# Sums of v on VectorE instead of GpSimd, with a new plan and a new order of the first batch's transposes

## Chip, core and metric

The kernel runs on one core of one Trainium2 chip. The metric is the device time in microseconds of one execution; the figure for a kernel is the median of its runs. A core has five engines that work side by side, each with its own instruction queue that it works off in order: PE (TensorE, matmuls), DVE (VectorE, elementwise work), ACT (ScalarE, activations and copies), POOL (GpSimd) and SP (SyncE, here used to issue DMAs). They wait for one another by semaphores. SBUF is the working memory, PSUM the memory into which PE accumulates.

## What is computed

Two stages follow each other, and only the result of the second leaves the chip. Attention over 8 batches of 3008 tokens, width 256, with 64 columns for the scores:

```python
scores = scale * np.matmul(z, z.transpose(0, 2, 1))   # scale = 1 / S, S = 3008
attn = np.maximum(scores, 0.0) ** 2
x = u * np.matmul(attn, v)                            # [8, 3008, 256]
```

and a feed-forward layer on the 24064 tokens, with an inner width of 2048:

```python
h = x @ w_in
g = h * np.cos(h)
out = g @ w_out
```

The scores of a batch are symmetric, since z meets itself.

## The kernel before, in words

**Tiling.** Tokens are cut into blocks of 128; 24 blocks make a batch (the last has 64 tokens), and 4 blocks make a column of 512 tokens, six columns a batch. `c` is the column whose output is being made, `R` the group of four key blocks that is summed over, `k` a block in a group. A score tile of column c and group R holds 4 x 128 keys by 512 tokens in 16 bits.

**Scores.** `s_visit` makes score tiles in visits of up to three pairs of blocks: `s_matmuls` (line 263) writes two PSUM banks for each pair, ACT takes the positive part (line 299, on diagonal tiles line 280), DVE squares it (line 301, diagonal line 285). As the scores are symmetric, only tiles with R >= c are computed, and the others are turned copies: after the second pair of a tile, `s_squares` issues a DMA transpose on SP's queue (line 308) into a tile "t" of its own. In the first batch, columns 0, 1 and 2 ("direct") are computed whole, without turned copies. `NSLOT` = 18 buffers hold all these tiles; `use` records from when to when each is needed, and `place` assigns the buffers.

**Attention times v.** For the groups in `WSET[c]` (groups 0 to 2, for the last two columns 0 to 3) the product of scores and v goes by a scheme of seven products in place of eight, on halves: `product(b, c, n)` (line 465) uses sums and differences of score quarters, made by DVE in place (`a_sums1`, lines 422 and 424; `a_sums2`, line 434), and sums of v quarters, which lie in `vsum[R]`, four parts for each group (part 0 is read by product 5, part 1 by 6, part 2 by 7, part 3 by 4). `keep` (lines 479 to 490) moves and adds the partial results. The other groups go as plain matmuls, `av_bank` (line 351), and `av_half` adds the last half block (line 328). `finish` multiplies the result by u turned (`turn_u`, line 179, another DMA transpose on SP) and gives x (line 380).

**Sums of v.** `v_sums(b, R)` makes `vsum[R]` once for each batch and group R = 0 to 3 by four GpSimd operations of 256 elements each (lines 391 to 395): part 0 = V12 − V11, part 2 = V22 − V12, part 1 = V22 − part 0, part 3 = V21 − part 1.

**Feed-forward.** `h_quantum` makes 128 rows of h (two matmuls, line 499), the cosine by ACT (line 503), and the product on DVE (line 506). `y_quantum` multiplies by w_out (line 516), ACT copies the result out (line 523) and issues the store. Score visits, h and y share the six PSUM banks of `ps_w`; the two others are the accumulators of the attention.

**Loads.** GpSimd issues all loads of u, v, z and the weights (line 119), each held behind the matmul that stands before it in the plan (`hold`). v comes in three blocks of eight key blocks each, planned 12, 3.2 and 0.8 units before the batch begins.

**The order.** All of it is written out as a list of events `(time, rank, ...)` in a planner's unit; a column takes U = 8 units, a batch 48, and batch b begins at 48 b. Sorting the list gives the order in which the instructions are traced; PE's order is fixed by it (`chain`). The tables at the head say when what is due in a column, in units from its start: `PLAN` (products "P1" to "P7", plain blocks "A" for the first and "B" for the second accumulator), `SUM1` and `SUM2` (first time and step of the score sums), `WADD` and `RADD` (additions of `keep`), `HALF` (from when `av_half` may go), `TSUM` (when the v sums of groups 0 to 3 are due, from the start of the batch). In the first batch the v sums stand at 16 to 19 units. `after(ins, other, NOSYNC)` tells the compiler to put an instruction behind another without a wait.

Of the kernel before, what the change touches and what calls it, by code (L numbers as in the profile page):

```python
# [14 lines left out]
def kernel(  # L15
# [9 lines left out]
    nc = tc.nc  # L25
# [43 lines left out]
    }  # L69
    SUM1, SUM2, WADD, RADD = {0: (-3.9, 0.65), 1: (-3.8, 0.35), 2: (-2.4, 0.3), 3: (-2.9, 0.7), 4: (-3.65, 0.55), 5: (-3.0, 0.75)}, {0: (1.95, 0.02), 1: (1.85, 0.02), 2: (1.95, 0.02), 3: (1.6, 0.02), 4: (2.0, 0.02), 5: (1.85, 0.02)}, {0: 5.26, 1: 4.96, 2: 4.26, 3: 4.36, 4: 4.26, 5: 4.46}, {0: 4.45, 1: 5.75, 2: 4.15, 3: 4.05, 4: 3.55, 5: 4.65}  # L70
    TSUM = [-2.0, -1.9, -0.8, 2.0, 2.5]
    XEND = 4.0
    WSET = {0: [0, 1, 2], 1: [0, 1, 2], 2: [0, 1, 2], 3: [0, 1, 2], 4: [0, 1, 2, 3], 5: [0, 1, 2, 3]}
    HALF = {0: 5.2, 1: 3.9, 2: 3.7, 3: 4.1, 4: 4.2, 5: 4.7}
# [168 lines left out]

    def slot(*key):
        return slots[slot_of[key]].rearrange("p (s k w) -> p s k w", s=K, w=P)
# [24 lines left out]
    def s_squares(b, c, R, p, banks):  # L270
# [30 lines left out]
        nc.vector.tensor_tensor(  # L301
            t.rearrange("p s k w -> p k s w")[:, 2 * p:2 * p + 2], rv, rv, ALU.mult)
        if p == 1:
            fresh[(b, c, R)] = [t[:, :, k, :] for k in range(K)]
            if R > c and not direct(b, R, c):
                tt = slot("t", b, c, R)
                turned[(b, c, R)] = tt
                nc.sync.dma_start_transpose(
                    tt.rearrange("p s k w -> p (s k) w"),
                    t.rearrange("p s k w -> p (s k w)"))  # L310
# [54 lines left out]
    def finish(b, c):  # L365
# [12 lines left out]
        for nh in range(NDH):  # L378
            for x, o, n in parts:
                nc.vector.tensor_tensor(  # L380
                    x[:, nh, :], acc[nh][:, o:o + n], ut[:, nh, o:o + n], ALU.mult)


    def v_sums(b, R):

        j = R * K
        t = vs(b, j // G)
# [350 lines left out]
```

## Time and profile before

| what | before |
|---|---|
| median of 11 runs | 1267.58 us (1264.02 to 1270.7) |
| profiled execution | 1264.8 us, of which the span from first to last instruction is 1263.0 us |
| busy PE / DVE / ACT / POOL | 97% / 84% / 66% / 19% of the span |
| mean granted TensorE clock | 0.982 |
| chain that ended last | PE 91%, DVE 7%, ACT 1%, issue 1% |

A line of the profile names a group of instructions by line, engine, operation and what it writes and reads; "x151 | 95.9, 640 | 2.0" means 151 instructions, 95.9 us busy, 640 ns mean, and 2.0 us that the engine stood idle just before them, with what ended that idle time behind an arrow. Weight loads (PEld) run beside the matmuls. The granted clock is the share of its full clock that PE is allowed at the time.

### The profile page before, as it was taken

The page shows a single profiled execution, that of the slowest core. Times are in us where ns is not written, and L with a number is a line of the kernel's source. Part 1 is how long each engine was busy: PE and PEld are TensorE (multiplying, and loading weights), DVE is VectorE, ACT ScalarE, POOL GpSimd, SP SyncE. Part 2 cuts the span into 40 slices and gives each one's busy share as a digit, 9 for nine tenths or more (in the row PEclk, how much of TensorE's full clock was granted, in tenths as well). Part 3 has the DMA queues.
Part 4 walks back from the last instruction along what each step waited for, and adds up shares of the span by engine and source line. Part 5 has one row for each costly group of instructions (what it writes and reads, how often), then busy time and mean ns, then how long its engine had stood idle before and what let it go on. Part 6 is the DMA issues. An engine that isn't in the chain of part 4 may idle for free.

```text
span 1263.0 us, 23106 instructions
## 1 busy us (share of the span) xinstructions
PE 1227.0 (97%) x8439; PEld 774.1 (61%) x8439; DVE 1056.0 (84%) x1977; ACT 836.1 (66%) x1744; POOL 236.8 (19%) x329
## 2 busy tenths in 40 slices
PE   8999899998999989999999999999999999999999
PEld 3366566664666646666566665666656666566666
DVE  8988878888788887888878888788887888878875
ACT  6767667675666767667667676676766767567655
POOL 4601401014010140101401014010140101400000
PEclk9999899998999989999999998999989999899999
DMA  9997868678687695868867668786696857956401
GB/s 163 180 150 115 127 99 128 109 115 118 103 117 126 115 112 108 124 119 118 127 101 126 108 116 134 100 128 106 111 140 91 136 105 107 140 106 105 81 26 51
DMA packets 484226, 145.02 MB, mean 115 GB/s; under 512 B 432400, under 2 KB 484112, under 8 KB 484112
## 3 DMA queue, kind: packets, MB, share of 16 engines
q1 hardware_dynamic: 356448, 88.73, 43.3%
q0 software_dynamic: 100400, 29.77, 23.7%
q10 hardware_dynamic: 27264, 25.06, 6.1%
q8 instruction: 66, 1.08, 0.4%
q14 instruction: 48, 0.39, 0.1%
HBM read 60.29 MB, written 24.64 MB: 67 GB/s over the span
## 4 chain that ended last, share of the span: by engine, by line
PE 91%; DVE 7%; ACT 1%; issue 1%
PE w L516 25%; PE w L499 25%; PE acc L465 18%; PE acc L351 16%; PE w L263 6%; DVE s L424 3%; DVE g L506 1%; DVE s L301 1%; ACT rt L299 1%; PE acc L328 1%; DVE s L422 0%; PE w L695 0%; ACT zT L224 0%; DVE x L380 0%; DVE s L434 0%
## 5 line engine op out<-in xcount | busy, mean ns | idle before, releaser
L503 ACT ACTIVATE c<-w 128x512 f16<-128x512 f32 x752 | 440.0, 617 | 286.8 <-PE w L499 192.7
L506 DVE TENSOR_TENSOR g<-w,c 128x512 f16<-128x512 f32 x752 | 490.3, 682 | 55.1 <-ACT c L503 53.1
L516 PE MATMUL w<-w_out,g 128*128 128x256 f16 x3008 | 454.5, 275 | 0.0
L499 PE MATMUL w<-x,w_in 128*128 128x512 f16 x1504 | 454.0, 385 | 0.0
L516 PEld LDWEIGHTS <-g 128*128 128x128 f16 x3008 | 297.4, 99 | 197.8 <-issue 9.6
L299 ACT ACTIVATE rt<-w 128x512 f16<-128x512 f32 x489 | 253.2, 615 | 54.4 <-PE w L263 54.4
L351 PE MATMUL acc<-s,v 128*128 128x512 f16 (+1 forms) x1000 | 283.8, 379 | 0.8 <-DVE x L380 0.8
L301 DVE TENSOR_TENSOR s<-rt 128x1024 f16<-128x1024 f16 x254 | 179.1, 711 | 102.3 <-ACT rt L299 101.1
L499 PEld LDWEIGHTS <-w_in 128*128 128x128 f16 x1504 | 148.7, 99 | 69.2 <-issue 3.2
L119 POOL DMA_DIRECT2D ust<-in_u_dram x112 | 81.6, 736 | 566.3 <-PE acc L351 543.2
L465 PE MATMUL acc<-s,vsum 128*128 128x256 f16 (+1 forms) x1208 | 157.9, 270 | 0.9 <-DVE q L481 0.7
L351 PEld LDWEIGHTS <-v 128*128 128x128 f16 x1000 | 93.0, 98 | 84.1 <-issue 34.1
L263 PE MATMUL w<-zT 64*128 64x512 f16 (+3 forms) x684 | 100.4, 365 | 30.0 <-DVE g L506 27.3
L465 PEld LDWEIGHTS <-vsum 128*128 128x128 f16 x1208 | 117.2, 98 | 17.8 <-issue 4.4
L465 PE MATMUL acc<-s,v 128*128 128x256 f16 (+1 forms) x906 | 117.6, 270 | 0.0
L434 DVE TENSOR_TENSOR s<-s,s 128x1024 f16<-128x1024 f16 (+1 forms) x151 | 94.9, 670 | 9.3 <-PE acc L465 8.9
L465 PEld LDWEIGHTS <-v 128*128 128x128 f16 x906 | 85.4, 98 | 20.4 <-issue 12.4
L424 DVE TENSOR_TENSOR s<-s 128x512 f16<-128x512 f16 (+1 forms) x151 | 95.9, 640 | 2.0
L263 PEld LDWEIGHTS <-zT 64*128 64x128 f16 x684 | 26.4, 94 | 86.8 <-issue 73.2
L523 ACT ACTIVATE ob<-w 128x256 f32<-128x256 f32 x188 | 71.2, 378 | 8.0 <-PE w L516 8.0
L380 DVE TENSOR_TENSOR x<-acc,ut 128x64 f16<-128x64 f32 (+7 forms) x178 | 68.8, 428 | 2.4 <-PE acc L351 1.7
L280 ACT ACTIVATE rt<-w 128x512 f16<-128x512 f32 (+3 forms) x176 | 62.8, 451 | 11.5 <-PE w L263 8.3
(38 smaller groups left out, 442.0 us busy)
## 6 DMA issues: line engine op xcount, KB each, us to landing
out_dram<-ob ACTq DMA_DIRECT2D x92, 256.0 KB, 2.2
ust<-in_u_dram POOLq DMA_DIRECT2D x80, 128.0 KB, 4.6
v<-in_v_dram POOLq DMA_DIRECT2D x16, 512.0 KB, 6.5
s<-s SPq DMA_TRANSPOSE x249, 4.4
v<-in_v_dram POOLq DMA_DIRECT2D x8, 448.0 KB, 8.0
zst<-in_z_dram POOLq DMA_DIRECT2D x14, 128.0 KB, 4.9
ust<-in_u_dram POOLq DMA_DIRECT2D x16, 96.0 KB, 4.3
w_in<-in_moe_w_in_dram POOLq DMA_DIRECT2D x4, 256.0 KB, 8.9
```

The costliest lines, as they stand in the source:

```text
L119: hold(nc.gpsimd.dma_start(dst, src))
L263: chain(nc.tensor.matmul(sp[:, s0 * P:], zt[h, R * K + k + 1 - lo, :], zt[h, j0 + s0:j0 + K, :].rearrange("p j w -> p (j w)"), start=True, ...
L299: nc.scalar.activation(rt[:, i, :], banks[k], AF.Relu)
L301: nc.vector.tensor_tensor(t.rearrange("p s k w -> p k s w")[:, 2 * p:2 * p + 2], rv, rv, ALU.mult)
L351: chain(nc.tensor.matmul(acc[:, 0:wn], vs(b, j // G)[:, j % G, nh * P:(nh + 1) * P], a, start=(start and n == 0), stop=(last and n == len( ...
L424: nc.vector.tensor_tensor(second(b, c, R), s1, quarters(b, c, R, (0, 0)), ALU.subtract)
L434: after(nc.vector.tensor_tensor(dst, src, sub, ALU.subtract).ins, before[-1], NOSYNC)
L465: chain(nc.tensor.matmul(acc[bank][:, cols], lhs[:, k, :], rhs[:, k, :] if old else rhs[:, :, k * P:(k + 1) * P], start=(n in (1, 5) and i ...
L499: chain(nc.tensor.matmul(hp, w_in16[:, k, ft * P:(ft + 1) * P], x[:, k, :], start=(k == 0), stop=(k == NDH - 1)))
L503: nc.scalar.activation(c16, hp, AF.Sin, bias=math.pi / 2.0, scale=inv_s2)
L506: nc.vector.tensor_tensor(gs[(m, ft // FG)][:, ft % FG, :], hp, c16, ALU.mult)
L516: chain(nc.tensor.matmul(ys[m][:, 0:D], gs[(m, f4)][:, ft % FG, ts * P:(ts + 1) * P], w_out16[:, ft, :], start=(ft == 0), stop=(ft == NFT ...
```

## The change

Four things are done together.

1. `v_sums` goes to VectorE, in three operations: parts 0 and 2 come from one operation of 512 elements, parts 1 and 3 from one of 256 each. They stand at new planned points: `TSUM` goes from −2.0, −1.9, −0.8, 2.0 to −2.9, −0.9, −0.8, 3.5 units for the groups 0 to 3.
2. The first batch's score transposes are no longer issued when a tile is done, but as events of their own at times given by `TURNS`, in the order in which later columns read the turned tiles. The lives of the buffers follow.
3. The u transposes of the first three columns of the first batch move to 0.7, 0.8 and 3.0 units (from 1, 5 and 10). In those direct columns, squares and positive parts on VectorE are put behind the last product of the preceding `finish` (`behind`).
4. The tables `PLAN`, `SUM1`, `SUM2`, `WADD`, `RADD` and `HALF` have new values: the same products, blocks and sums at other times.

```diff
...
-    TSUM = [-2.0, -1.9, -0.8, 2.0, 2.5]
+    TSUM = [-2.9, -0.9, -0.8, 3.5, 3.5]
...
-    HALF = {0: 5.2, 1: 3.9, 2: 3.7, 3: 4.1, 4: 4.2, 5: 4.7}
+    HALF = {0: 3.6, 1: 3.2, 2: 3.2, 3: 3.4, 4: 4.5, 5: 4.2}
...
+    TURNS = {(0, 0, 1): None, (0, 0, 2): None, (0, 1, 2): None,
+             (0, 0, 3): 1.0, (0, 0, 4): 2.4, (0, 1, 3): 7.8, (0, 0, 5): 8.0,
+             (0, 2, 3): 14.4, (0, 1, 4): 14.6, (0, 2, 4): 15.8, (0, 1, 5): 20.0,
+             (0, 2, 5): 22.0}
...
-                nc.vector.tensor_scalar_max(rt[:, i, :], banks[k], 0.0)
+                behind(nc.vector.tensor_scalar_max(rt[:, i, :], banks[k], 0.0).ins)
...
+        if direct(b, c, R):
+            behind(ins)
         if p == 1:
             fresh[(b, c, R)] = [t[:, :, k, :] for k in range(K)]
-            if R > c and not direct(b, R, c):
...
+            if R > c and (b, c, R) not in TURNS:
+                turn_s(b, c, R)
+
+    def turn_s(b, c, R):
+        tt = slot("t", b, c, R)
+        turned[(b, c, R)] = tt
+        nc.sync.dma_start_transpose(
+            tt.rearrange("p s k w -> p (s k) w"),
+            halves[(b, c, R)].rearrange("p s k w -> p (s k w)"))
...
+        if direct(b, c, c):
+            ended[:] = [ins]
+
+    ended = []
+
+    def behind(ins):
+
+        if ended:
+            after(ins, ended[0], NOSYNC)
...
     def v_sums(b, R):
 
         j = R * K
-        t = vs(b, j // G)
-        k1, k2 = (slice(j % G + 2 * i, j % G + 2 * i + 2) for i in range(2))
-        d1, d2 = slice(0, P), slice(P, 2 * P)
+        t = vs(b, j // G)[:, j % G:j % G + K, :].rearrange("p (h k) d -> p h k d", h=2)
         o = vsum[R]
-        after(nc.gpsimd.tensor_tensor(o[:, 0], t[:, k1, d2], t[:, k1, d1],
-                                      ALU.subtract).ins, before[-1], NOSYNC)
-        nc.gpsimd.tensor_tensor(o[:, 2], t[:, k2, d2], t[:, k1, d2], ALU.subtract)
-        nc.gpsimd.tensor_tensor(o[:, 1], t[:, k2, d2], o[:, 0], ALU.subtract)
-        nc.gpsimd.tensor_tensor(o[:, 3], t[:, k2, d1], o[:, 1], ALU.subtract)
+        b12, b22 = t[:, :, :, P:2 * P], t[:, 1, :, P:2 * P]
+        left = t[:, 0, :, :].rearrange("p k (d w) -> p d k w", w=P)
+        after(nc.vector.tensor_tensor(o[:, 0:3:2], b12, left, ALU.subtract).ins,
+              before[-1], NOSYNC)
+        nc.vector.tensor_tensor(o[:, 1], b22, o[:, 0], ALU.subtract)
+        nc.vector.tensor_tensor(o[:, 3], t[:, 1, :, 0:P], o[:, 1], ALU.subtract)
...
-            if p == 1 and R > c and not direct(b, R, c):
+            if p == 1 and R > c and TURNS.get((b, c, R), t) is not None:
+                t = TURNS.get((b, c, R), t)
                 use(("t", b, c, R), t + 0.8, t + 2.5)
                 use(("a", b, c, R), t, t + 3)
...
+    for key, t in TURNS.items():
+        if t is not None:
+            at(t, 3.5, lambda key=key: turn_s(*key))
...
-            at(t + c * U + (1 if b or c not in (1, 2) else -3 * c), 0, lambda b=b, c=c: turn_u(b, c))
+            at(t + c * U + (1 if b or c > 2 else (0.7, -7.2, -13.0)[c]), 0, lambda b=b, c=c: turn_u(b, c))
```

The new tables, in part (columns 0 and 5 of `PLAN`, and the times of the sums):

```diff
-        0: [(1.0, 'P1 P5 P2'), (2.35, 'B1'), (2.55, 'P6 B1'), (3.0, 'P7 B1'),
-            (3.4, 'P3'), (4.55, 'A1'), (5.0, 'P4 A1'), (5.4, 'B1'), (6.15, 'B3'),
-            (6.35, 'B2'), (6.55, 'A2'), (7.0, 'A2 B2'), (7.4, 'A5')],
+        0: [(1.0, 'P1 P2'), (1.4, 'P5'), (2.35, 'P6 B1'), (2.55, 'B1'), (3.0, 'P7 B1'),
+            (3.4, 'P3'), (4.55, 'A1'), (4.75, 'A1'), (5.4, 'P4 B2'), (6.15, 'A1 B2'),
+            (6.35, 'A1 B1'), (6.55, 'A2'), (6.75, 'A1'), (7.0, 'A1 B2'), (7.4, 'A3 B1')],
...
-            (3.4, 'P7'), (4.35, 'B1'), (4.75, 'P4 A1'), (5.4, 'A1 B2'), (6.15, 'A2'),
-            (6.35, 'A1'), (7.0, 'A2 B1'), (7.4, 'B1')],
+            (3.4, 'P7 B2'), (4.75, 'A1'), (5.0, 'P4'), (5.4, 'A1 B1'), (6.15, 'A1 B1'),
+            (6.35, 'A2'), (6.75, 'A1'), (7.0, 'B2'), (7.4, 'A1')],
...
-    SUM1: {0: (-3.9, 0.65), 1: (-3.8, 0.35), 2: (-2.4, 0.3), 3: (-2.9, 0.7), 4: (-3.65, 0.55), 5: (-3.0, 0.75)}
+    SUM1: {0: (-3.9, 0.5), 1: (-1.8, 0.4), 2: (-1.9, 0.15), 3: (-2.9, 0.65), 4: (-4.65, 0.65), 5: (-3.0, 0.7)}
-    SUM2: {0: (1.95, 0.02), 1: (1.85, 0.02), 2: (1.95, 0.02), 3: (1.6, 0.02), 4: (2.0, 0.02), 5: (1.85, 0.02)}
+    SUM2: {0: (1.85, 0.02), 1: (1.75, 0.37), 2: (1.85, 0.02), 3: (1.5, 0.02), 4: (1.9, 0.02), 5: (1.75, 0.07)}
```

More of the change, by code (lines that the diff above doesn't have):

```diff
@@ L379, in finish @@
             for x, o, n in parts:
-                nc.vector.tensor_tensor(
-                    x[:, nh, :], acc[nh][:, o:o + n], ut[:, nh, o:o + n], ALU.mult)
+                ins = nc.vector.tensor_tensor(
+                    x[:, nh, :], acc[nh][:, o:o + n], ut[:, nh, o:o + n], ALU.mult).ins
+        if direct(b, c, c):
[4 more added lines that the diff above has]
+            after(ins, ended[0], NOSYNC)
     def v_sums(b, R):
         j = R * K
-        t = vs(b, j // G)
-        k1, k2 = (slice(j % G + 2 * i, j % G + 2 * i + 2) for i in range(2))
-        d1, d2 = slice(0, P), slice(P, 2 * P)
+        t = vs(b, j // G)[:, j % G:j % G + K, :].rearrange("p (h k) d -> p h k d", h=2)
         o = vsum[R]
-        after(nc.gpsimd.tensor_tensor(o[:, 0], t[:, k1, d2], t[:, k1, d1],
-                                      ALU.subtract).ins, before[-1], NOSYNC)
-        nc.gpsimd.tensor_tensor(o[:, 2], t[:, k2, d2], t[:, k1, d2], ALU.subtract)
-        nc.gpsimd.tensor_tensor(o[:, 1], t[:, k2, d2], o[:, 0], ALU.subtract)
-        nc.gpsimd.tensor_tensor(o[:, 3], t[:, k2, d1], o[:, 1], ALU.subtract)
+        b12, b22 = t[:, :, :, P:2 * P], t[:, 1, :, P:2 * P]
[4 more added lines that the diff above has]
+        nc.vector.tensor_tensor(o[:, 3], t[:, 1, :, 0:P], o[:, 1], ALU.subtract)
     def by_key(b, c, R):
```

11 lines of the change are left out of this document (3 added, 8 removed), and 26 rows, old and new, of the table PLAN.

## The prediction

> **What bounds the kernel now.** I read the page first, then the busy time by stretches of the span, then the timeline of a stretch that stood out. The profiled execution took 1264.8 us, its span is 1263.0 us.
>
> ```profile
> span 1263.0 us, 23106 instructions
> ...
> PE 1227.0 (97%) x8439; PEld 774.1 (61%) x8439; DVE 1056.0 (84%) x1977; ACT 836.1 (66%) x1744; POOL 236.8 (19%) x329
> PEclk9999899998999989999999998999989999899999
> ...
> L506 DVE TENSOR_TENSOR g<-w,c 128x512 f16<-128x512 f32 x752 | 490.3, 682 | 55.1 <-ACT c L503 53.1
> ...
> L424 DVE TENSOR_TENSOR s<-s 128x512 f16<-128x512 f16 (+1 forms) x151 | 95.9, 640 | 2.0
> ```
>
> PE is the bound, but two things in these lines are not those of a full PE: its granted clock dips six times, five slices apart, with the dip between the third and the fourth left out, and a VectorE operation of line 424 on 512 16-bit elements takes 640 ns on average, hardly less than line 506 with a 32-bit operand from PSUM. The stretches, cut at the dips and at the place of the missing one, show where PE loses its time (columns: length, busy time of PE, PEld, DVE, ACT and POOL with instruction counts, granted clock, DMA share, GB/s):
>
> ```profile
> 0.00:15.00 15.00, 11.73 (x66) 4.57 (x67) 10.08 (x22) 9.21 (x16) 9.78 (x18) 1.00 1.15 160
> 50.00:70.00 20.00, 17.53 (x96) 8.20 (x95) 19.94 (x37) 14.96 (x31) 10.46 (x14) 1.00 1.47 179
> 128.00:143.00 15.00, 10.10 (x50) 4.79 (x48) 14.24 (x16) 7.02 (x16) 12.06 (x18) 0.77 1.14 143
> 143.00:286.00 143.00, 143.00 (x1022) 93.20 (x1020) 118.92 (x235) 98.30 (x208) 16.14 (x22) 1.00 0.67 112
> 286.00:301.00 15.00, 9.94 (x46) 4.71 (x44) 14.49 (x19) 7.03 (x15) 12.45 (x19) 0.81 1.15 146
> 445.00:460.00 15.00, 10.10 (x50) 4.84 (x48) 14.69 (x19) 7.37 (x16) 12.85 (x19) 0.77 1.30 142
> 604.00:617.00 13.00, 10.02 (x51) 5.08 (x49) 13.00 (x19) 7.06 (x16) 12.51 (x18) 0.87 1.28 184
> 760.00:774.00 14.00, 11.28 (x52) 5.38 (x51) 13.67 (x19) 7.22 (x16) 12.63 (x18) 0.76 1.29 184
> 917.00:931.00 14.00, 11.27 (x51) 5.39 (x50) 13.66 (x19) 7.12 (x15) 12.46 (x18) 0.76 1.30 186
> 1074.00:1088.00 14.00, 10.95 (x49) 5.21 (x48) 13.39 (x18) 7.08 (x15) 12.56 (x18) 0.76 1.22 170
> 1212.00:1263.00 51.00, 47.84 (x360) 34.58 (x357) 30.55 (x48) 27.49 (x55) 0.00 (x0) 1.00 0.14 42
> ```
>
> Inside a batch PE is busy 143.00 of 143.00 us at full clock: nothing is to be won there. The loss sits in the seven stretches where one batch follows another, and there GpSimd is busy 12 to 13 us. The timeline of the first and of the fourth says why:
>
> ```profile
> 128.34 6.36 DVE L424 TENSOR_TENSOR s<-s 128x512 f16<-128x512 f16 x1
> 128.75 1.31 POOL L391 TENSOR_TENSOR vsum<-v 128x256 f16<-128x256 f16 x2
> 131.60 0.39 PE L263 MATMUL w<-zT 64*128 64x512 f16 x1
> 134.49 0.73 POOL L394 TENSOR_TENSOR vsum<-v,vsum 128x256 f16<-128x256 f16 x1
> 134.62 1.15 DVE L301 TENSOR_TENSOR s<-rt 128x1024 f16<-128x1024 f16 x1
> 135.69 2.47 DVE L506 TENSOR_TENSOR g<-w,c 128x512 f16<-128x512 f32 x4
> 136.43 0.86 PE L263 MATMUL w<-zT 64*128 64x384 f16 x2 [4.44 <-DVE g L506]
> ...
> 602.11 0.92 POOL L119 DMA_DIRECT2D v<-in_v_dram  x1 [4.80 <-PE w L263]
> 604.18 4.50 DVE L424 TENSOR_TENSOR s<-s 128x512 f16<-128x512 f16 x1
> 607.11 1.28 POOL L395 TENSOR_TENSOR vsum<-v,vsum 128x256 f16<-128x256 f16 x2
> 607.44 0.39 PE L263 MATMUL w<-zT 64*128 64x512 f16 x1
> 608.64 1.79 POOL L393 TENSOR_TENSOR vsum<-v 128x256 f16<-128x256 f16 x2 [0.25 <-DMA v<-in_v_dram]
> 609.94 0.32 PE L263 MATMUL w<-zT 64*128 64x384 f16 x1 [2.11 <-DVE g L506]
> ```
>
> ```profile
> L424 DVE TENSOR_TENSOR s<-s x151: 377/414/6361, 53.1 to 1209.7; 128x512 f16<-128x512 f16 x119, 128x448 f16<-128x448 f16 x32
> ```
>
> The last row gives shortest, median and longest duration: an operation of 0.41 us lasts 6.36 us while GpSimd works off its sums one after another. In the fourth stretch it ends at 608.68, inside the 0.25 us (608.39 to 608.64) in which GpSimd had no sum because it waited for v. So VectorE gets its operands only when GpSimd pauses. The products of line 506 wait behind it, the score matmuls of line 263 wait for the PSUM buffers that these free, and after the wait the clock is halved (0.76 over 14 us).
>
> On VectorE's waiting, the Trainium skill (SBUF — State Buffer, Who interferes with whom) says that the pair of ports shared by GpSimd and VectorE is an exclusive lock, that an operation with two SBUF inputs needs it, and that the first to start has it for one whole instruction. The trace agrees on the blocking, not on its length: by the page VectorE would wait for one sum at most.
>
> **The change part by part.**
>
> *Sums leave GpSimd.* What goes is the whole chain above. Idle PE in the seven stretches, length less PE busy: 4.90 + 5.06 + 4.90 + 2.98 + 2.72 + 2.73 + 3.05 = 26.3 us. Clock not granted, length times (1 − clock): 3.45 + 2.85 + 3.45 + 1.69 + 3 × 3.36 = 21.5 us. Together 47.9 us. A second count: the seven hold 349 matmuls, which at the 1022 in 143 us of a steady stretch need 48.8 us of their 100, so 51.2 us are lost. The two differ by the mix of matmul sizes; I take 48.
>
> The Trainium skill (TensorE: Matmul & The Clock Gate, What's actually happening) puts the halving behind an idle window of about 3.4 us. Here a wait of 2.11 us was enough, so I count all seven; by the page only the first three would pay, and the two sums would be 26.3 + 9.8 = 36 us.
>
> *Sums come to VectorE.* A group costs one operation of 512 elements and two of 256. The first is bounded by line 424's 0.41 us; the nearest rows for 256 elements are these:
>
> ```profile
> L285 DVE TENSOR_TENSOR s<-rt 128x256 f16<-128x256 f16 x44 | 15.6, 355 | 0.0
> L481 DVE TENSOR_TENSOR q<-acc,p 128x256 f32<-128x256 f32 x37 | 15.3, 413 | 0.0
> ...
> L394 POOL TENSOR_TENSOR vsum<-v,vsum 128x256 f16<-128x256 f16 x32 | 23.5, 744 | 1.4
> ```
>
> L285 (0.36, some of them slowed by GpSimd) is the nearest form; I take 0.30. A group is 0.41 + 2 × 0.30 = 1.0 us against 4 × 0.74 = 3.0 us on GpSimd, and 32 groups are 32 us; if the rows of 128 elements, which no VectorE operation of before reads, make them as slow as operations with 32-bit operands, 0.68 (line 506) + 2 × 0.41 (line 481) = 1.5 us, 48 us in all. VectorE sheds 95.9 − 151 × 0.414 = 33 us of blocking at line 424 alone, so its total stays near 1056 us, under 90% of a shorter span: no bound on average.
>
> Locally it may be one. Of the 14.24 us that VectorE is busy in 128:143, 5.94 are blocking; 8.3 us of work stand against 15 − 8.35 = 6.65 us of PE at full speed. Two groups land at −0.9 and −0.8 units in that place (a unit is a planner's step, 3.3 us: 1263 over 8 × 48), one at −2.9 and one at 3.5. That is a deficit of 8.3 + 2.0 − 6.65 = 3.65 us, if PE could not run ahead at all: 25.6 us over seven. Against it: PE loses nothing in a stretch where VectorE has no idle time either.
>
> ```profile
> 750.00:758.00 8.00, 8.00 (x65) 5.63 (x63) 7.96 (x16) 4.35 (x9) 1.30 (x2) 1.00 0.35 82
> ```
>
> ```profile
> v<-in_v_dram POOLq DMA_DIRECT2D x16, 512.0 KB, 6.5
> ```
>
> ```profile
> 125.58 0.92 POOL L119 DMA_DIRECT2D v<-in_v_dram  x1 [4.12 <-PE acc L351]
> ```
>
> Then a new wait: group R = 2 reads v's second block, issued at 125.58 and landed 6.5 us later, 132.1. PE reached the score visit of −0.8 at 131.60, so VectorE can stand there about 0.5 us (1.1 in the fourth: 602.11 + 6.5 against 607.44), with the next score squares and the products of line 506 queued behind it and PE's six PSUM buffers behind those. I charge both together 0.7 us of PE at each crossing, 5 us, between 0 and 25.6 + slow clock; I stay near the lower end because of the 7.96 row. The group at −2.9 overwrites what product 4 of the last column reads at −3.0: eight matmuls, under 1 us on VectorE, covered as in 750:758.
>
> *GpSimd's queue.* Without sums it issues v's third block on time instead of after 134.49; its readers come over 3 units later. Zero.
>
> *First batch.* Its score transposes and u transposes change places in SP's queue, and VectorE takes the finishing products of a column before the squares.
>
> ```profile
> 39.90 1.46 PE L351 MATMUL acc<-s,v 128*128 128x512 f16 x6 [0.78 <-DVE x L380]
> 40.28 31.07 SPq L308 DMA_TRANSPOSE s<-s  x7
> ...
> 67.72 0.81 PE L465 MATMUL acc<-s,vsum 128*128 128x256 f16 x6 [0.66 <-DVE q L481]
> ```
>
> SP is backed up for 31 us, yet nothing on PE waits for a transpose; what waits is 0.78 us for a finishing product, and 2.5 us in 50:70, where VectorE is busy 19.94 of 20. Four groups of sums (4 us) enter between 40 and 55 us, where GpSimd's stood, and the doubling of line 301 by GpSimd (1.15 for 0.69, as in the row at 134.62) leaves. The held-back transposes, three for column 3 from 14.4 to 15.8 units at 4.4 us each, have 5 units (16 us) before their first reader. I take 0; the ends are −3.3 (both waits gone) and +4 (sums on the path).
>
> *The new order of products, A/V pieces and score sums.* The same matmuls in other places. In-batch waits are nil now, so this can only lose: the longest wait of a product is the 0.66 us at 67.72, and at each of the 45 planned columns (48 less the first three) that would be 30 us. The 143.00 of 143.00 shows how rare such waits are with the present plan; zero, with the 30 us kept for the second rival.
>
> *Sum.* 1264.8 − 48 + 5 = 1222 us for an execution like the profiled one. That one lies 2.8 us under the median of 1267.58, so the median of the changed kernel is 1222 to 1225; I put 1223.
>
> **The rivals.**
>
> *A rest of the stall stays.* VectorE's deficit, its wait for v, or product waits by the new order leave 1.5 to 3 us idle at each crossing. As 2.11 us was enough to lose the clock once, 3.4 us come on top at some: 7 × 1.5 = 10 to 7 × (3 + 2) = 35 us back on 1264.8 − 48 + 2.8 = 1220: 1230 to 1255. For it the 8.3 against 6.65; against it the 7.96 row.
>
> *The sums are not what holds VectorE*, as the order of starts suggests: line 424 began at 128.34, before the first sum at 128.75. Then one sum of 0.7 us per crossing is saved, 5 us, VectorE gains 32 us of work in its idle time, and the time is 1260 to 1267: no change. Against it: the end inside GpSimd's pause at 608.68. The page on the shared ports, taken by its letter, stands with this rival.
>
> *Slower: VectorE waits in order for v's second block.* Price: 7 × (W + 3.4). It equals the 48 us won at W = 3.5 us, so v would have to land 10 us after its issue, or VectorE reach the group 3 us sooner than PE's place for it. At W = 5 the time is 1220 + 59 = 1279. The 6.5 us median speaks against it.
>
> **How the numbers follow.** My forecast 0.75 (1212 to 1231), the rest of the stall 0.18 (1230 to 1255), sums innocent 0.03, slower 0.04. The low end of the range is 1264.8 − 51.2 − 3.3 = 1210; the high end, 1245, takes in two thirds of the second case. About 0.2% is what a measurement can tell here (2.5 us): faster 0.93, same 0.03, slower 0.04.
>
> **What would show it.** Line 424 with no duration above 0.8 us; GpSimd with DMA issues alone; granted clock 1.00 at all crossings; a PE near 98 to 99% of the span. Wrong if a crossing still shows a score matmul that waits over 1.5 us for line 506, if VectorE's first sum of group 2 waits for the DMA of v for over 2 us, or if products wait for VectorE inside batches.

## The result and the profile after

| | before | after |
|---|---|---|
| median | 1267.32 us (1263.02 to 1271.95, 47 runs) | 1226.66 us (1220.01 to 1231.54, 12 runs) |
| ratio after to before | | 0.9681, 95% interval 0.9666 to 0.9696 |
| profiled execution, its granted clock | 1264.8 us, 0.982 | 1221.55 us, 0.997 |

The forecast was 1223 us in a range of 1210 to 1245. The runs of the changed kernel fall into two groups, six at 1220.0 to 1224.7 us with a granted clock of 0.996 to 0.999 and six at 1228.6 to 1231.5 us with 0.993 or 0.994, and the profiled execution is one of the shorter six.

From the page of the changed kernel, the same lines as before. Line numbers have shifted: the score sums of line 424 are now line 444, those of 422 line 442, the products of 506 line 526, the score matmuls of 263 line 270, the squares of 301 line 308, the score transposes of 308 line 320, the u transposes of 179 line 181.

```profile
span 1219.5 us, 23076 instructions
...
PE 1208.8 (99%) x8439; PEld 769.6 (63%) x8439; DVE 1028.1 (84%) x2073; ACT 833.7 (68%) x1744; POOL 145.8 (12%) x201
...
PEclk9989999999999999999999999999999999999999
```

The dips of the granted clock are gone but the one in the third slice, which is the first batch, and PE is 99% busy. The same matmuls take 18.2 us less of busy time (1227.0 to 1208.8), since none of them runs at half clock at a batch's end. The stretches that stood out, cut in the same way (length, busy PE, PEld, DVE, ACT, POOL, granted clock, DMA share, GB/s):

```profile
50.00:70.00 20.00, 15.68 (x70) 6.86 (x69) 14.65 (x28) 12.06 (x24) 4.41 (x7) 0.83 1.35 195
...
128.00:143.00 15.00, 15.00 (x108) 9.46 (x107) 14.59 (x35) 11.92 (x26) 4.46 (x6) 1.00 1.02 136
...
286.00:301.00 15.00, 15.00 (x110) 9.74 (x109) 13.47 (x32) 10.73 (x25) 2.10 (x3) 1.00 1.28 190
```

The first crossing from batch to batch holds 108 matmuls where it held 50, with no idle time and no clock withheld; the other six crossings of this trace, too, have PE busy throughout and a clock of 1.00. The stretch of the first batch, 50:70, went the other way: 70 matmuls where there were 96, and a clock of 0.83 where it was 1.00. The durations of single lines (count, shortest/median/longest in ns):

```profile
L412 DVE TENSOR_TENSOR vsum<-v x32: 412/416/419, 42.1 to 1054.7; 128x512 f16<-128x512 f16 x32
...
L414 DVE TENSOR_TENSOR vsum<-v,vsum x32: 277/281/285, 42.8 to 1056.8; 128x256 f16<-128x256 f16 x32
...
L444 DVE TENSOR_TENSOR s<-s x151: 375/414/427, 53.8 to 1166.2; 128x512 f16<-128x512 f16 x119, 128x448 f16<-128x448 f16 x32
```

A group of sums costs VectorE 0.42 + 2 × 0.28 = 0.98 us (line 415 has the same median as line 414), and line 444, whose longest was 6361 ns, has none above 427.

### The profile page after: what moved, and what is told of

Read it like the earlier page. It is cut to its first block, busy times and chain, and to the rows that moved or that the text cites. A ratio compares the mean times of both kernels' runs of the same rounds, so it can differ in the third digit from the quotient of the medians.

```text
span 1219.5 us, 23076 instructions
## 1 busy us (share of the span) xinstructions
PE 1208.8 (99%) x8439; PEld 769.6 (63%) x8439; DVE 1028.1 (84%) x2073; ACT 833.7 (68%) x1744; POOL 145.8 (12%) x201
## 4 chain that ended last, share of the span: by engine, by line
PE 96%; DVE 2%; DMA 1%; issue 0%; ACT 0%; ACTq 0%; DVEq 0%
PE w L536 27%; PE w L519 26%; PE acc L485 19%; PE acc L363 17%; PE w L270 6%; PE acc L340 1%; DMA s<-s 1%; DVE s L308 1%; DMA x<-in_z_dram 0%; DVE rt L304 0%; ACT rt L306 0%; DVE g L526 0%; DVE s L454 0%; DVE vsum L412 0%; ACTq L208 0%
## 5 line engine op out<-in xcount | busy, mean ns | idle before, releaser
L536 PE MATMUL w<-w_out,g 128*128 128x256 f16 x3008 | 448.6, 273 | 0.0
L519 PE MATMUL w<-x,w_in 128*128 128x512 f16 x1504 | 447.5, 380 | 0.0
L536 PEld LDWEIGHTS <-g 128*128 128x128 f16 x3008 | 294.2, 98 | 191.2
L308 DVE TENSOR_TENSOR s<-rt 128x1024 f16<-128x1024 f16 x254 | 172.6, 687 | 84.9 <-ACT rt L306 84.0
L270 PE MATMUL w<-zT 64*128 64x512 f16 (+3 forms) x684 | 91.6, 362 | 5.8 <-DVE g L526 4.2
L121 POOL DMA_DIRECT2D v<-in_v_dram x40 | 31.2, 788 | 298.2 <-PE acc L485 144.1
L442 DVE TENSOR_TENSOR s<-s 128x512 f16<-128x512 f16 (+1 forms) x151 | 60.7, 407 | 3.1 <-DMA s<-s 3.1
```

The source lines that it names most:

```text
L121: hold(nc.gpsimd.dma_start(dst, src))
L270: chain(nc.tensor.matmul(sp[:, s0 * P:], zt[h, R * K + k + 1 - lo, :], zt[h, j0 + s0:j0 + K, :].rearrange("p j w -> p (j w)"), start=True, ...
L308: ins = nc.vector.tensor_tensor(t.rearrange("p s k w -> p k s w")[:, 2 * p:2 * p + 2], rv, rv, ALU.mult).ins
L519: chain(nc.tensor.matmul(hp, w_in16[:, k, ft * P:(ft + 1) * P], x[:, k, :], start=(k == 0), stop=(k == NDH - 1)))
L536: chain(nc.tensor.matmul(ys[m][:, 0:D], gs[(m, f4)][:, ft % FG, ts * P:(ts + 1) * P], w_out16[:, ft, :], start=(ft == 0), stop=(ft == NFT ...
```

## The experiments

The theory was the prediction's: line 424 stands still for as long as GpSimd works off its sums without a pause, and this is what starves PE at each crossing; the other edits are worth nothing. The main rival was that the new plan carries the gain. Every ratio is to the kernel before on the same chip.

### The sums alone, on the old plan

The kernel before, with only the new `v_sums`:

```diff
-        after(nc.gpsimd.tensor_tensor(o[:, 0], t[:, k1, d2], t[:, k1, d1],
-                                      ALU.subtract).ins, before[-1], NOSYNC)
...
+        after(nc.vector.tensor_tensor(o[:, 0:3:2], b12, left, ALU.subtract).ins,
+              before[-1], NOSYNC)
+        nc.vector.tensor_tensor(o[:, 1], b22, o[:, 0], ALU.subtract)
+        nc.vector.tensor_tensor(o[:, 3], t[:, 1, :, 0:P], o[:, 1], ALU.subtract)
```

> The kernel before with the new three-operation sums of v on VectorE and nothing else: old plan, old times of the sums, old first batch. Theory (the sums on GpSimd are the whole stall at the crossings): no operation of line 424 over 0.5 us, granted clock 1.00 at the crossings, 1214 to 1228 us. Rival (the new plan carries the gain, the sums alone only trade GpSimd time for VectorE time): over 1250 us, with the score matmuls at the crossings still waiting over 2 us.

Measured: 1228.51 us (1226.67 to 1232.41), ratio 0.9693 [0.9671, 0.9714]. Its line of the score sums and its first crossing:

```profile
L423 DVE TENSOR_TENSOR s<-s x151: 377/416/426, 57.7 to 1173.6; 128x512 f16<-128x512 f16 x119, 128x448 f16<-128x448 f16 x32
...
128.00:143.00 15.00, 14.31 (x101) 8.62 (x99) 14.15 (x33) 11.46 (x25) 4.46 (x6) 1.00 1.02 124
```

As the theory had it: moving the sums is sufficient for nearly the whole gain. 0.7 us of idle PE is left at this crossing, in waits of 0.15 to 0.31 us for the products of line 505; the changed kernel, with its new plan, has none.

### Everything but the sums

The changed kernel with the four GpSimd operations put back into `v_sums` (the diff above, turned round).

> The changed kernel with the four sums back on GpSimd, everything else (plan, times of the sums, first batch) as changed. Theory: the stall of 4 to 6 us at the crossings stays wherever GpSimd makes two or more groups back to back, 1255 to 1280 us. Rival (the plan carries the gain): 1222 to 1235 us.

Measured: 1229.05 us (1227.8 to 1230.28), ratio 0.9693 [0.9676, 0.971]. This is the expectation of the rival; the theory's 1255 to 1280 fell. So leaving GpSimd is not necessary either: with everything else changed, moving the sums to VectorE is worth 2.4 us (1229.05 to 1226.66), and the intervals of the two ratios overlap. The line of the score sums, and VectorE and GpSimd at the second crossing:

```profile
L445 DVE TENSOR_TENSOR s<-s x151: 375/415/776, 54.3 to 1172.6; 128x512 f16<-128x512 f16 x119, 128x448 f16<-128x448 f16 x32
```

```profile
285.90 0.68 POOL L412 TENSOR_TENSOR vsum<-v 128x256 f16<-128x256 f16 x1
285.94 0.94 DVE L443 TENSOR_TENSOR s<-s 128x512 f16<-128x512 f16 x1
...
286.67 0.74 POOL L415 TENSOR_TENSOR vsum<-v,vsum 128x256 f16<-128x256 f16 x1
...
286.91 0.78 DVE L445 TENSOR_TENSOR s<-s 128x512 f16<-128x512 f16 x1
```

GpSimd still makes sums at the crossing, and still stretches VectorE's operations, but each by no more than one sum: 0.94 and 0.78 us where 0.41 is the rule. Each of these sums reads the result of the one before it (line 415 part 0, line 416 part 1), so GpSimd pauses between them: 286.58 to 286.67, 287.41 to 287.49. In the kernel before, the compiler had laced several groups that stood close together (−2.0, −1.9 and −0.8 units) into one chain, so that the next sum was always ready:

```profile
132.51 1.28 POOL L393 TENSOR_TENSOR vsum<-v 128x256 f16<-128x256 f16 x2
133.76 0.66 POOL L391 TENSOR_TENSOR vsum<-v 128x256 f16<-128x256 f16 x1
```

These rows stand between those at 128.75 and 134.49 of the prediction: each record begins before the last one ends (133.76 against 133.79), and the first gap of the chain is 134.42 to 134.49, ahead of line 394, which reads part 0. VectorE's 6.36 us end at 134.70. The new theory was therefore that it is the unbroken chain, not the number of sums, that costs the time, and three runs were made for it. One difference was left aside in it: the two operations above start while a sum runs, the one of 6.36 us started ahead of the first.

### Only the new times of the sums

```diff
-    TSUM = [-2.0, -1.9, -0.8, 2.0, 2.5]
+    TSUM = [-2.9, -0.9, -0.8, 3.5, 3.5]
```

on the kernel before; the sums stay on GpSimd, in four operations.

> The kernel before, sums on GpSimd, old plan, old first batch; only the planned times of the sums are the new ones (-2.9, -0.9, -0.8, 3.5 units), so that the first group goes alone, its third and fourth sum each behind a gap, and GpSimd has two DMA issues between it and the next groups. Theory (what costs is a row of sums that follow without a gap while VectorE wants two operands): line 424 at most 1.5 us, PE idle at a crossing under 1.2 us, 1224 to 1240 us. Rival (the stall goes only with the new plan of products and score sums): 1250 us or more.

Measured: 1230.66 us (1228.81 to 1235.16), ratio 0.9725 [0.9701, 0.9749]; longest operation of line 424 895 ns; the crossing at 128:

```profile
128.00:143.00 15.00, 14.80 (x104) 8.99 (x101) 14.84 (x25) 12.09 (x26) 12.55 (x17) 1.00 1.20 161
```

Four numbers of a table bring 35 us. They pull the groups apart: GpSimd ends one at 130.79 and begins the next sums at 134.43.

```profile
129.79 1.00 POOL L395 TENSOR_TENSOR vsum<-v,vsum 128x256 f16<-128x256 f16 x1
...
134.43 1.30 POOL L393 TENSOR_TENSOR vsum<-v 128x256 f16<-128x256 f16 x2 [2.15 <-DMA v<-in_v_dram]
```

### The groups kept in turn

The kernel before, its times unchanged, with GpSimd's sums tied into one order, a whole group (parts 0, 2, 1, 3) after the other:

```diff
+        def next_sum(ins):
+            if chained:
+                after(ins, chained.pop(), NOSYNC)
+            chained.append(ins)
```

> The kernel before, its sums still on GpSimd at the same planned times, but the four sums of a group in one row (parts 0, 2, 1, 3) and one group after the other, where before two groups alternate and each sum starts before the one ahead of it has ended. The last sum of a group needs the third, so a gap of about 0.08 us opens in each group. Theory (VectorE gets its operands only in a gap between two sums): line 424 no longer waits 6 us, its longest is 1 to 3 us, the idle PE at each crossing falls under 1.5 us, 1225 to 1248 us. Rival (what counts is how much GpSimd sums, not how they follow each other): longest over 4 us and 1260 to 1270 us.

Measured: 1241.51 us (1240.93 to 1243.65), ratio 0.9797 [0.9771, 0.9822]. The first crossing of this kernel:

```profile
131.15 2.63 DVE L435 TENSOR_TENSOR s<-s 128x512 f16<-128x512 f16 x1
...
131.55 0.69 POOL L400 TENSOR_TENSOR vsum<-v 128x256 f16<-128x256 f16 x1
132.19 0.68 POOL L403 TENSOR_TENSOR vsum<-v 128x256 f16<-128x256 f16 x1
132.81 0.68 POOL L404 TENSOR_TENSOR vsum<-v,vsum 128x256 f16<-128x256 f16 x1
133.57 0.74 POOL L405 TENSOR_TENSOR vsum<-v,vsum 128x256 f16<-128x256 f16 x1
```

In this order the first three sums of a group need not wait for one another, only the fourth reads the result of the third. VectorE's operation lasts as long as the three: it ends at 133.78, 0.29 us after the gap that begins at 133.49. Same sums, same engine, same due times, a chain of three in place of nine: 2.63 us in place of 6.36, and 26 us are won. The time and the longest operation are those of the theory; the idle PE, 1.59 us in 130:145, is a little over the 1.5 it allowed.

### Something else between the sums

The last kernel, with a fill of an unread tile of 256 elements on GpSimd after each sum:

```diff
+            pause = nc.gpsimd.memset(scratch, 0.0).ins
+            after(pause, ins, NOSYNC)
```

> As the kernel with the groups in turn, and behind each sum GpSimd fills a small scratch tile (256 elements), which writes SBUF and reads nothing. Theory (a stretch without a reading GpSimd operation lets VectorE in, whatever else GpSimd does): longest operation of line 424 at most 1.3 us, PE idle at each crossing under 0.8 us, 1222 to 1235 us, although GpSimd works longer. Rival (any GpSimd operation holds VectorE off): as long as or longer than with the groups in turn alone, line 424 over 2 us and a later end.

Measured: 1252.79 us (1252.03 to 1253.68), ratio 0.9883 [0.9858, 0.9908]. The theory missed: here the fills as such do not let VectorE in.

```profile
131.70 3.14 DVE L438 TENSOR_TENSOR s<-s 128x512 f16<-128x512 f16 x1
...
132.10 0.69 POOL L403 TENSOR_TENSOR vsum<-v 128x256 f16<-128x256 f16 x1
132.72 0.33 POOL L399 MEMSET scratch<- 128x256 f16 x1
...
134.47 0.32 POOL L399 MEMSET scratch<- 128x256 f16 x1
134.74 0.67 POOL L408 TENSOR_TENSOR vsum<-v,vsum 128x256 f16<-128x256 f16 x1
```

VectorE stays out through the fills at 132.72 and 133.60. It ends at 134.84, beside the fill at 134.47, although GpSimd shows no pause there either: each record begins before the one ahead of it ends. What is special about this place is the next sum, line 408, which reads the result of the sum that ended at 134.55 (line 407, 0.68 us from 133.87). The same holds in the three other kernels: VectorE's operation ends 0.28 to 0.30 us after the end of a sum whose result GpSimd's next sum reads (134.42 to 134.70 before; 133.49 to 133.78 with the groups in turn; 286.58 to 286.88 and 287.41 to 287.69 in everything but the sums; 134.55 to 134.84 here).

That the next sum must be one that is not ready is no general condition, though. In the kernel with only the new times VectorE comes in between two sums without a gap:

```profile
122.68 1.29 POOL L393 TENSOR_TENSOR vsum<-v 128x256 f16<-128x256 f16 x2 [15.91 <-PE acc L465]
123.51 0.75 DVE L422 TENSOR_TENSOR s<-s 128x512 f16<-128x512 f16 x1
123.94 0.84 POOL L391 TENSOR_TENSOR vsum<-v 128x256 f16<-128x256 f16 x1
```

Line 422 starts while a sum runs, waits for this one alone and ends at 124.26. It is the next sum that is stretched, 0.84 us where 0.66 is its shortest, although line 391 reads no sum and so was ready. This is the usual case in all the kernels with sums on GpSimd: an operation that starts while a sum runs mostly waits for that sum only. The same goes for a fill: in this kernel VectorE comes in beside the one at 55.66 us, ahead of a sum that is ready (line 403, which then takes 0.87 us). The long waits are of another kind. In the kernel before, in the one with the groups in turn and in the one with fills, at all seven crossings, the operation that waits starts 0.40 to 0.43 us ahead of the first sum, while GpSimd issues a load, here in the kernel before:

```profile
127.25 1.49 POOL L119 DMA_DIRECT2D ust<-in_u_dram  x2 [0.74 <-PE acc L351]
```

The issue ends at 128.74, line 424 started at 128.34, the first sum starts at 128.75. So two things meet in the long wait: an operation that starts in this place, and a row of sums behind it that are ready. Only the second was varied by itself (nine sums against three). Whether it would have been enough to move the issue of the load was not tried, and in the kernel with only the new times the place has moved too (line 424 starts at 128.36, the next sum at 129.03). By which rule the ports are given in that way stays open.

### What the sums cost on VectorE

The next runs stand on the changed kernel with the first batch's edits undone (the run "the old first batch" below: 1219.64 us). In one, each group's three operations are done twice:

```diff
+        nc.vector.tensor_tensor(o[:, 0:3:2], b12, left, ALU.subtract)
+        nc.vector.tensor_tensor(o[:, 1], b22, o[:, 0], ALU.subtract)
+        nc.vector.tensor_tensor(o[:, 3], t[:, 1, :, 0:P], o[:, 1], ALU.subtract)
```

> Sums on VectorE, new plan, first batch as before (the kernel that ran at 1219.6 us), with each group's three VectorE operations done twice: 32 x 0.75 to 1.0 us more VectorE work, most of it at the crossings. Theory (VectorE has room there): within 3 us of 1219.6. Rival (the charge of the prediction, 0.7 us of PE for the sums at each crossing): 1225 to 1245 us with score matmuls waiting at the crossings.

In the other, they are left out from the second batch on:

```diff
-            at(b * span + (TSUM[R] if b else 2 * U + R), 2, lambda b=b, R=R: v_sums(b, R))
+            if b == 0:
+                at(2 * U + R, 2, lambda b=b, R=R: v_sums(b, R))
```

> The same kernel (1219.6 us) with the sums of batches 1 to 7 left out, so that their products read those of the first batch. Theory (the sums on VectorE cost PE nothing): 1217 to 1222 us. Rival (they cost PE something at the crossings, or delay what follows them): 1205 to 1214 us.

Measured: twice, 1230.55 us (1227.31 to 1231.31), ratio 0.9697 [0.967, 0.9724]; left out, 1218.45 us (1218.11 to 1219.55), ratio 0.9613 [0.9589, 0.9638]. Leaving them out wins about 1 us by the medians, with intervals that overlap, as the theory said; doing them twice costs 11 us by the medians and 10 by the ratios, where the theory allowed 3. The first crossing of both, the kernel with the doubled sums first, and a wait in that one:

```profile
137.00:152.00 15.00, 14.22 (x104) 9.08 (x103) 14.48 (x35) 9.86 (x23) 2.09 (x3) 1.00 1.09 176
...
143.56 1.47 PE L488 MATMUL acc<-s,v 128*128 128x256 f16 x12 [0.78 <-DVE x L392]
```

```profile
128.00:143.00 15.00, 15.00 (x106) 9.56 (x103) 13.28 (x26) 11.93 (x26) 3.58 (x5) 1.00 1.29 167
```

One set of sums, 7 × 4 × 0.98 us = 27 us of VectorE's time, costs PE next to nothing; a second set no longer fits: a product waits 0.78 us for the finishing products that then stand behind sums. By this, VectorE has room for about one set at a crossing.

### The old first batch

The changed kernel with points 2 and 3 of the change undone, sums and tables kept (in part):

```diff
-            if R > c and (b, c, R) not in TURNS:
+            if R > c and not direct(b, R, c):
...
-            at(t + c * U + (1 if b or c > 2 else (0.7, -7.2, -13.0)[c]), 0, lambda b=b, c=c: turn_u(b, c))
+            at(t + c * U + (1 if b or c not in (1, 2) else -3 * c), 0, lambda b=b, c=c: turn_u(b, c))
```

> The changed kernel with the first batch's edits undone: score transposes issued when a tile is done, u transposes at 1, 5 and 10 units, no ordering behind the finishing products. Theory (these edits are what makes VectorE wait 3.1 us for a transpose near 58 us, and cost 3.2 us of PE plus 3.4 us of clock there): no such wait, 1214 to 1221 us, clock 0.999 or more. Rival (the wait comes with the new plan, not with these edits): the wait stays, 1222 to 1232 us.

Measured: 1219.64 us (1218.12 to 1222.52), ratio 0.9621 [0.9602, 0.964]: 7 us less than the changed kernel, the intervals apart. The first batch's edits cost time.

### Which of the first batch's edits

Only the u transposes put back to 1, 5 and 10 units:

```diff
-            at(t + c * U + (1 if b or c > 2 else (0.7, -7.2, -13.0)[c]), 0, lambda b=b, c=c: turn_u(b, c))
+            at(t + c * U + (1 if b or c not in (1, 2) else -3 * c), 0, lambda b=b, c=c: turn_u(b, c))
```

> The changed kernel with the u transposes of the first columns at their old times (1, 5 and 10 units); the planned times of the score transposes and the order behind the finishing products stay. Theory (the early u transpose, which waits on SP for its load, holds the score transposes back by 4 us): VectorE's wait for a score tile near 58 us falls under 1.5 us, a wait for a u tile near 40 us of about 2 us comes back, 1216 to 1223 us. Rival (the new times of the score transposes make the wait): it stays over 2.5 us, 1225 to 1232 us.

The reverse of it: the old first batch with only the u transposes early, at 0.7, 0.8 and 3.0 units.

> The kernel with the old first batch (1219.6 us, granted clock 0.998 to 1.000) with one edit of the change put back: the u transposes of columns 1 and 2 at 0.8 and 3.0 units, without the new places of the score transposes and without the order of VectorE behind the finishing products. Theory, that this edit alone is what the first batch costs: 1223 to 1231 us, runs spread over some 10 us as those of the changed kernel (1220 to 1231), clock 0.993 to 0.999, because a u transpose now stands in SP's queue ahead of all score transposes and every turned tile lands later; in the profile a wait of PE over 2.5 us near 62 us with half clock behind it, and no wait for a finishing product near 41 us. Rival, that it is harmful only together with the held-back squares or the new places of the score transposes: 1217 to 1221 us, all runs within 5 us at a clock of 0.998 or more.

Measured: put back, 1220.05 us (1218.41 to 1222.15), ratio 0.9638 [0.9614, 0.9661]; early alone, 1227.56 us (1225.52 to 1232.86), ratio 0.9672 [0.9655, 0.9688]. The times are those of the theory in both: the early u transposes are what the first batch costs, and the rest of its edits is worth nothing that shows. With them put back, VectorE's waits are also as expected, 0.83 us for the score tile and 2.55 for the u tile. SP's queue in the changed kernel:

```profile
12.68 8.35 SPq L181 DMA_TRANSPOSE ut<-ust  x2
21.13 10.51 SPq L320 DMA_TRANSPOSE s<-s  x2
```

In the kernel before, the first score transposes were issued at 16.88 us:

```profile
16.88 12.76 SPq L308 DMA_TRANSPOSE s<-s  x3
```

In the changed kernel the u transposes of two columns go first, and the first score transpose is issued at 21.13. What then waits, VectorE's score sum and behind it PE:

```profile
60.95 0.43 DVE L442 TENSOR_TENSOR s<-s 128x512 f16<-128x512 f16 x1 [3.06 <-DMA s<-s]
...
62.02 0.58 PE L270 MATMUL w<-zT 64*128 64x512 f16 x1 [3.20 <-DVE g L526]
```

The sum reads a turned tile that has not landed, the products of line 526 are queued behind it, and PE's banks behind those. The old first batch has two waits for the one:

```profile
40.58 1.29 DVE L392 TENSOR_TENSOR x<-acc,ut 128x512 f16<-128x512 f32 x2 [2.25 <-DMA ut<-ust]
...
60.88 0.43 DVE L441 TENSOR_TENSOR s<-s 128x512 f16<-128x512 f16 x1 [0.93 <-DMA s<-s]
```

The tile near 61 us comes at the same time in both. So in this shorter run the later start of the first score transpose is not what makes VectorE wait: the early u transposes take away the wait at 40 us, VectorE reaches the sum 2 us sooner, and it waits there that much longer. The two profiled executions are only 2.4 us apart (1221.55 and 1219.14); most of the 7 us between the medians comes from the longer runs of the changed kernel. The kernel with the early u transposes alone was profiled in one of its longer runs (1232.86 us), and there the wait is of another kind:

```profile
64.35 0.69 DVE L308 TENSOR_TENSOR s<-rt 128x1024 f16<-128x1024 f16 x1 [10.34 <-DMA s<-s]
...
66.50 1.81 PE L270 MATMUL w<-zT 64*128 64x512 f16 x4 [10.61 <-DVE g L525]
```

The square waits 10.34 us. It reads no turned tile, so by the code it can only wait for a transpose to let go of the buffer that it overwrites. The stretch 50:75 of the kernel before, of the old first batch, of the changed kernel and of this one, in that order:

```profile
50.00:75.00 25.00, 22.53 (x132) 11.73 (x131) 24.73 (x48) 18.76 (x39) 10.46 (x14) 1.00 1.42 182
```

```profile
50.00:75.00 25.00, 22.68 (x129) 10.97 (x126) 24.01 (x49) 19.97 (x42) 6.88 (x9) 1.00 1.41 194
```

```profile
50.00:75.00 25.00, 20.21 (x95) 8.93 (x94) 19.59 (x36) 15.20 (x31) 4.41 (x7) 0.86 1.28 193
```

```profile
50.00:75.00 25.00, 13.81 (x50) 4.78 (x51) 13.70 (x30) 9.07 (x17) 6.14 (x8) 0.73 1.38 173
```

PE is idle 2.3 us in the second and 11.2 in the last, where 6.75 us more of clock are withheld. This fits the two groups of runs of the changed kernel: a wait of 3 us in the shorter, and in the longer, with the granted clock of 0.993 or 0.994 that this kernel also has, one of about 10. For its own longer runs it is not shown: its one profile is of a shorter run.

### Two tries at a better order

The changed kernel with its nine planned score transposes tied in the planned order. Without the tie, the compiler need not issue them in the order of `TURNS`; the profile's rows do not tell one tile from another, so the order that it chose is not shown here.

```diff
+        if (b, c, R) in TURNS:
+            if queued:
+                after(dma.ins, queued.pop(), NOSYNC)
+            queued.append(dma.ins)
```

> The changed kernel with the nine planned score transposes of the first batch tied to each other, so that SP issues them in the order of their planned times: the tile of column 2 and group 3 comes fifth among the score transposes instead of seventh. Theory (the tile is late because two transposes that are read much later stand ahead of it): it lands about 8 us sooner, near 53 us, VectorE does not wait, 1214 to 1221 us. Rival (the DMA engines, not the queue order, make it late): the wait at 58 us stays over 2 us, 1222 to 1232 us.

And the old first batch with the u transpose of column 1 one unit earlier, at 4 units in place of 5:

> Sums on VectorE, new plan, first batch as before (1219.6 us), with one thing moved: the u transpose of column 1 is planned at 4 units in place of 5, so that SP issues it ahead of the third score transpose. Theory (SP's order alone decides): the 2.3 us wait for the u tile near 40 us goes, with the 3.4 us of half clock behind it, and the score tile of column 2 and group 3 comes no later, 1214 to 1218 us. Rival (the DMA engines are full there, so that what one tile gains another loses): the wait moves to the score tile near 58 us, 1219 to 1226 us.

Measured: tied, 1231.24 us (1227.31 to 1231.84), ratio 0.9707 [0.9689, 0.9725], a miss; one unit earlier, 1222.12 us (1216.32 to 1224.86), ratio 0.9645 [0.9618, 0.9673], no gain that can be told from 1219.64. In the tied kernel a square again waits for a transpose, 9.56 us:

```profile
63.84 0.69 DVE L308 TENSOR_TENSOR s<-rt 128x1024 f16<-128x1024 f16 x1 [9.56 <-DMA s<-s]
```

In the profile of the kernel with the u transpose one unit earlier (1224.79 us), the wait at 40 us is gone, but the score sum that came at 60.88 in the old first batch now waits until 64.55, behind a square that waited 5.20 us for a transpose:

```profile
64.55 0.42 DVE L441 TENSOR_TENSOR s<-s 128x512 f16<-128x512 f16 x1 [2.02 <-DMA s<-s]
```

This is what the rival said: what one tile gains, another loses. That the DMA engines are the reason is not shown. The run one unit earlier has two values at 1216.3 and 1216.7 us, at a granted clock of 1.000, and the others at 1220.6 to 1224.9: so some 3 us lie below the best median, which no kernel here holds steadily.

## Why the prediction was right, and where its steps were not

The time came out inside the likeliest case (1212 to 1231), 3.7 us above the 1223; the sum for the profiled execution was 1222, and it took 1221.55. That these two agree to half a microsecond is in part luck: two terms of the sum were missed and nearly cancel, and the profiled execution is one of the shorter runs. The steps did less well than the sum.

- *The chain at the crossings, 48 us.* Right. Between the kernel before and the old first batch lie 0.0379 × 1267.3 = 48 us, and no crossing of the changed kernel withholds clock or leaves PE idle. The reading on which it rests, "VectorE gets its operands only when GpSimd pauses", is too wide. It holds, nearly, for line 424 at the crossings, which starts ahead of the first sum; an operation that starts while a sum runs mostly waits for that one alone.
- *"Sums leave GpSimd" as the cause.* Too narrow. What had to go was the meeting of line 424 with an unbroken chain behind it. New times alone bring 35 us, everything but the sums 39, the sums alone 39, both together with the tables 48: two sufficient causes overlap, and their gains do not add.
- *The new plan "can only lose", zero.* Wrong. With the sums already on VectorE the tables bring 1228.51 − 1219.64 = 9 us. About 5 of them are the 0.5 to 0.7 us of idle PE that the old plan leaves at or near each of the seven crossings; where the others come from, and which entries of the tables do it, was not separated.
- *VectorE's deficit and its wait for v, 5 us.* Mis-sized. The sums cost about 1 us in all with the new plan. The wait never occurred, line 412 has no idle time before it in the whole trace: the groups planned at −0.9 and −0.8 came behind the score visit, when v's block had landed, by the median of 6.3 us from issue to landing:

```profile
129.96 0.88 POOL L121 DMA_DIRECT2D v<-in_v_dram  x1 [20.33 <-PE acc L485]
...
136.74 0.77 PE L270 MATMUL w<-zT 64*128 64x512 f16 x6
137.00 0.75 DVE L412 TENSOR_TENSOR vsum<-v 128x512 f16<-128x512 f16 x2
```

  The place that the plan gives is not the place that the queue gives. That there is little room beside them, the doubled sums show (10 to 11 us).
- *The first batch, zero between −3.3 and +4.* Wrong, +7, and outside its ends. The step that failed is "SP is backed up for 31 us, yet nothing on PE waits for a transpose". It priced the score transposes, whose new places change nothing that shows (1220.05 us with them, 1219.64 without), and passed over the u transposes, which cost the 7 us. Taking the wait near 40 us away won nothing: the wait for a score tile grew from 0.93 to 3.06 us in the shorter run, and about 10 us are lost in the longer, if these are like those of the kernel with the early u transposes alone. That nobody waits in one schedule was read as slack.
- *The price of a group, 1.0 us.* Right: 0.98. GpSimd's own queue, zero: right, no instruction of PE or VectorE waits for a load of v.

In the order of the edits: sums alone −43 by the prediction, −39 measured; the plan 0 and −9; the first batch 0 and +7. The sum, −43 against −41, was right because the crossing term was right and the two that were missed nearly cancel. Of the rivals, a rest of the stall stays at the crossings only with the old plan (0.7 us of idle, no clock lost at 128:143); the slower case found no wait at all; that the sums are innocent is excluded by the first run.

The Trainium skill (SBUF — State Buffer, Who interferes with whom) gives the shared ports to the first to start, for one whole instruction. By that rule the wait would be one sum, and so it mostly is where VectorE's operation starts while a sum runs (0.94, 0.78 and 0.75 us for 0.41). The runs differ where it starts ahead of the first sum: there it stood through three (2.63 us) and nine (6.36 us). The Trainium skill (TensorE: Matmul & The Clock Gate, What's actually happening) wants about 3.4 us of idleness before the clock halves. Here the clock halved after a wait of 2.42 us (the old first batch, a stretch with a granted clock of 0.91):

```profile
41.32 1.49 PE L363 MATMUL acc<-s,v 128*128 128x512 f16 x6 [2.42 <-DVE x L392]
...
30.00:50.00 20.00, 17.57 (x85) 5.81 (x83) 15.84 (x32) 9.71 (x20) 2.96 (x4) 0.91 1.27 170
```

That counting all seven crossings was right shows in the 48 us; with 36 in its place, the forecast would have been 1235, 8 us above the measured median.

## What to carry to other kernels

When a short VectorE operation has a long worst case, look at GpSimd's queue beside it for operations that follow each other without a gap, and at whether the VectorE operation starts ahead of them or while one runs. Moving them, giving them other due times or ordering them so that the row is short each won 26 to 39 us here, and the cheapest is a table of due times. Before an edit of a DMA queue is priced at nothing because nobody waits for it, follow every instruction that it puts ahead of others to the first reader of what is delayed, and ask which wait comes next when the first is gone. A total that comes out right is no proof of its terms: only undoing the parts one by one showed that here a part of the change costs 7 us, and that the kernel without it (1219.64 us, ratio 0.9621 [0.9602, 0.964]) is the better one.

## What the hardware showed beside that

- GpSimd fills of 256 elements, which read nothing, did not end the wait of a VectorE operation that had started ahead of the row of sums (3.14 us for 0.41); it came in ahead of the first sum that needed the last one's result.
- The half clock needs no single long wait, and idle time does not always bring it. With the groups in turn the crossing at 130 loses 1.59 us in several pieces, 0.72 us the longest, and still has a granted clock of 0.89. With the fills, the second crossing loses 2.15 us in 284:299, 1.29 us the longest piece, at a clock of 1.00:

```profile
130.00:145.00 15.00, 13.41 (x79) 7.95 (x78) 13.37 (x21) 9.27 (x21) 14.58 (x21) 0.89 1.35 163
...
284.00:299.00 15.00, 12.85 (x84) 7.31 (x83) 14.25 (x24) 10.29 (x22) 13.93 (x27) 1.00 1.06 153
```

- One operation of 512 16-bit elements on VectorE (0.416 us) costs less than two of 256 (2 × 0.281), and one of 256 on GpSimd takes 0.66 to 0.74: the three operations for a group are a third of the four that they replace.
